# Batch 0's second exchange: by transposes for 8 of 32 m, through DRAM for the other 24

## The chip, the cores and the metric

One core of a Trainium2 chip runs the whole program. It has five engines that the profile names: TensorE (PE, with its weight loads as PEld), VectorE (DVE), ScalarE (ACT), GpSimd (POOL) and SyncE (SP, which only issues DMAs), and 16 DMA engines that all DMA queues share. PSUM, where TensorE writes, has eight banks of 2 KB for each of 128 partitions; only TensorE, VectorE and ScalarE reach it. The metric is the device time of one execution in microseconds (us), smaller is better.

## The reference, cut to what matters

```python
x:  (8, 3072, 256)            # batch, sequence, channel
X = rfft(x, axis=1);  Y = X * (filt_r + 1j * filt_i);  y = irfft(Y, n=3072, axis=1)
h = y.reshape(24576, 256)
g = maximum(h @ w1, h @ w2)   # (24576, 1024)
out = g @ w_out               # (24576, 256)
```

The Fourier transform of 3072 points is done as 96 times 32 with matrix products: sequence index = 32 p + m, with p from 0 to 95 and m from 0 to 31.

## The kernel before, in words

For each of the eight batches there are four matrix stages and then the feed-forward part.

- S1 contracts over p: the 96 rows of x are multiplied by the table C1 (`f1`, `s1`, and for batch 0 `s1t`). Its result has 96 rows, which are 24 frequencies u times 4 parts q.
- First exchange: from rows (u, q) and columns (m, d) to rows (q, m), 128 of them, for each u.
- S2 (`s2`) contracts over those 128 rows with the table U, for two pairs of u at a time: v = 0 to 5, each v covers four u and gives two PSUM banks px. `product` multiplies px with the filter F, giving two tiles pq for each v.
- S3 (`s3`) goes back with the tables VP and VQ, giving pz in rows (q, m) again.
- Second exchange: from rows (q, m) for each u to 96 rows (u, q) with columns (m, d), the tile zr.
- S4 (`s4`) contracts over the 96 rows with G1, for four m at a time, and leaves y transposed, with the channel on the partitions. One s4 makes one block tt of 384 tokens; a batch has eight blocks, and block i needs m = 4i to 4i+3.
- `moe_h` multiplies a block by Wd = w1 - w2 in eight steps j and takes the maximum with zero; `moe_o` multiplies the result by Wo and y by M = w2 Wo and adds them (max(a, b) = max(a - b, 0) + b).

For batches 1 to 7 both exchanges go through DRAM: `f1` or `s1` stores ad, and `f1_read` or `s1_read` reads it back as bt; `s3` stores zd, `z_read` reads it back as zr. For batch 0 both exchanges use TensorE transposes: `s1t` gives the result of S1 with the channel on the partitions, and `t1` turns it back as bt; `s3t` gives S3 with the channel on the partitions, as the tile zT with all 32 m, and `t2` turns four m of it at a time into zr.

The order of the work is written out by hand. First comes the opening: the tables (C1, U, VP, VQ) are made on the chip, x of batch 0 and the filter are loaded through GpSimd's queue, the second half of the filter's rows is doubled by VectorE (v below 4) or by DMA on SyncE's queue (v = 4, 5), and batch 0 goes through S1, S2, the products and S3. GpSimd makes some of the products (for s = 1 of v = 0, 2, 3, 4 and half of v = 5) from copies that ScalarE puts in SBUF (`stage_x`); after them stand on its queue the loads of batch 1's x, `prep_wd(0)` for Wd, the load of Wo (`load_wo`), another load of x and `prep_wd(1)`. Loads of w1 and w2 are on SyncE's queue. Matrix products of ones (`spin`, and one at the head of each `s3t`) fill waits of TensorE.

Then the main loop runs 64 steps for each batch, step = 8 tt + j. A step holds `moe_h(tt, j)`, a `visit` to the next batch from the list `mid` (S3 of the v before, S2 of this v, some S1 of the batch after next), about four products of `moe_o(tt - 1)`, and then whatever `todo` lists: f1, f1_read, t2, z_read, load_xf (x of a later batch, on SyncE's queue), fold (adds and subtracts its halves, GpSimd), casts and transposes of w2 (steps 3 to 7) and `prep_m` (step 8). At j = 4 (or 6 in the last block of a batch) the next block's s4 is issued, so s4(2) stands in step 12, s4(4) in step 28 and s4(8), the first of batch 1, in step 62.

Before, batch 0's t2 for c = 0 runs ahead of step 0, for c = 1 in step 2, and for c = 2 to 7 in steps 8, 16, 24, 32, 40 and 48. f1 for batch 1 runs once ahead of step 0 and 15 times in steps 0 to 12; f1_read stands in step 13, and batch 1's seven visits in steps 24, 28, 31, 35, 38, 42 and 46. Six PSUM banks belong to the pool ps and two to pso for the whole program. pq tiles come from pqpool (six) for v up to 2 and from pq0 (six more) for v from 3.

Of the kernel before, what the change touches and what calls it, by code (L numbers as in the profile page):

```python
# [8 lines left out]
FP32 = mybir.dt.float32  # L9
# [17 lines left out]
def kernel(  # L27
# [30 lines left out]
    zT = const.tile([128, 2, NM, NU, 4], BF16)  # L58
# [9 lines left out]
    ps = ctx.enter_context(tc.tile_pool(name="ps", bufs=6, space=bass.MemoryType.PSUM))  # L68
    pso = ctx.enter_context(tc.tile_pool(name="pso", bufs=2, space=bass.MemoryType.PSUM))
# [3 lines left out]
    pq0 = setup.enter_context(tc.tile_pool(name="pq0", bufs=6))  # L73
# [68 lines left out]

    V.memset(W1, 1.0)
# [3 lines left out]
    kc = init.tile([NP, NW, 2, 2], FP32)  # L147
    kap = init.tile([128, NW, 2], FP32)
# [3 lines left out]
    hv = init.tile([128, 2, 1], FP32)  # L152
    load_x(0, 0, 1)
    G.iota(pid, pattern=[[1, 1]], base=0, channel_multiplier=1, allow_small_or_imprecise_dtypes=True)
    G.iota(kc, pattern=[[2, NW], [24, 2], [1, 2]], base=0, channel_multiplier=0,
           allow_small_or_imprecise_dtypes=True)
    load_x(0, 1, 1)
    G.iota(kap, pattern=[[2, NW], [24, 2]], base=0, channel_multiplier=0,
# [4 lines left out]
    for c in range(3, 8):  # L163
        load_x(0, c, 1)
    for q in range(2):
        G.memset(hv[:, q], 1.0)
        for r in (0, 32):
            G.memset(hv[r:r + 1, q], 0.5 * (1 - q))
    load_f(0)
    load_f(1)  # L170
# [3 lines left out]
    def table_c():  # L174
        p96 = init.tile([128, 1], FP32)
        V.tensor_scalar(p96, pid, 1.0 / 96.0, None, OP.mult)
        uc = init.tile([NP, 48, 2], FP32)
        rc = init.tile([NP, 48, 2], FP32)
        kf = kc.rearrange("p w g s -> p (w g s)")
        V.tensor_scalar(uc[:, :, 0], kf, p96[0:NP], 0.25, OP.mult, OP.add)  # L180
        V.tensor_scalar(uc[:, :, 1], kf, p96[0:NP], None, OP.mult)
        V.tensor_scalar(uc[:, 0:1, 1], pid[0:NP], 0.5, 0.25, OP.mult, OP.add)
        V.tensor_scalar(rc, uc, RND, RND, OP.add, OP.subtract)
        V.tensor_tensor(uc, uc, rc, OP.subtract)
        S.activation(C1, uc.rearrange("p k r -> p (k r)"), AF.Sin, bias=zero[0:NP], scale=TWO_PI)
# [10 lines left out]
    def tables_u():  # L196
# [24 lines left out]
        V.tensor_scalar(t1[:, 0], kap.rearrange("p w g -> p (w g)"), a_, base, OP.mult, OP.add)  # L221
# [19 lines left out]
    def sines_u(h):  # L241
        uv = ua.rearrange("p u c s j -> p u (c s j)")
        S.activation(U[:, NW * h:NW * h + NW], uv[:, NW * h:NW * h + NW], AF.Sin, bias=zero, scale=TWO_PI)

    def table_g():
        pg = ps.tile([96, NP], FP32, tag="ps", name="pg")
        TE.matmul(pg, C1, I128[0:NP, 0:NP], start=True, stop=True)
        S.activation(G1, pg, AF.Copy)

    def table_v(h, q):  # L250
        pool, tag = (pso, "po") if h else (ps, "ps")
        pv = [pool.tile([128, 6, 64], FP32, tag=tag, name="pv%d" % s) for s in range(2)]
        for i in range(6):
            for g in range(2):
                for s in range(2):
                    rows = slice(64 * s, 64 * s + 64)
                    u = 2 * (6 * h + i) + g
                    if q == 0:
                        TE.matmul(pv[s][64 * g:64 * g + 64, i], U[rows, u], I128[rows, rows], start=True, stop=True)
                    else:  # L260
                        TE.matmul(pv[s][64 * g:64 * g + 32, i], U[rows, u, 32:64], I128[rows, rows],
                                  start=True, stop=True)
                        TE.matmul(pv[s][64 * g + 32:64 * g + 64, i], U[rows, u, 0:32], NI[rows, rows],
                                  start=True, stop=True)
        return pv

    def put_v(h, q, pv):
        for s in range(2):
            i0 = 1 if h == 0 and s == 0 else 0
            tab = VQ if q else VP  # L270
            if i0:
                S.activation(tab[:, 0, 0], pv[0][:, 0], AF.Identity, bias=zero, scale=hv[:, q])
            S.activation(tab[:, 6 * h + i0:6 * h + 6, s], pv[s][:, i0:6], AF.Copy)  # L273
# [96 lines left out]

    def s2(b, v):
        px = [ps.tile([128, 2, D], FP32, tag="ps", name="px%d" % s) for s in range(2)]
        for i in range(2):
            for s, g in ((0, 0), (1, 1), (0, 1), (1, 0)):
                u = 2 * (2 * v + i) + g
                TE.matmul(px[s][64 * g:64 * g + 64, i], U[64 * s:64 * s + 64, u], bt[b][64 * s:64 * s + 64, u],  # L376
                          start=True, stop=True)
        return px
# [12 lines left out]

    def s3(b, v, pq):
        if v == 0:
            zd[b] = dram.tile([NU, 128, D], BF16, tag="zd", name="zd")
        pz = [ps.tile([128, 2, D], FP32, tag="ps", name="pz%d" % g) for g in range(2)]
        for i in range(2):
            for q, tab in enumerate((VP, VQ)):
                for g, s in ((0, 0), (1, 1), (0, 1), (1, 0)):
                    TE.matmul(pz[g][64 * s:64 * s + 64, i], tab[64 * g:64 * g + 64, 2 * v + i, s],  # L399
                              pq[s][64 * g:64 * g + 64, q, i], start=(q == 0), stop=(q == 1))  # L400
        zt = zpool.tile([128, 2, 2, D], BF16, tag="zt", name="zt")
        for g in range(2):
            S.activation(zt[:, :, g], pz[g], AF.Copy)  # L403
        nc.sync.dma_start(out=zd[b][4 * v:4 * v + 4].rearrange("u p d -> p u d"),
                          in_=zt.rearrange("p i g d -> p (i g) d"))
# [89 lines left out]
    def s1t(c):  # L495
        for dc in range(2):
            pa = ps.tile([128, 4, 96], FP32, tag="ps", name="pa")
            for m in range(4):
                TE.matmul(pa[:, m], xb[0, c][:, m, 128 * dc:128 * dc + 128], C1, start=True, stop=True)
            o_ = at2[:, dc].rearrange("p u q m -> p (u q) m")[:, :, 4 * c:4 * c + 4]  # L500
            i_ = pa.rearrange("p m q -> p q m")
            if dc == 1 and c >= 6:
                V.tensor_copy(o_, i_)
            else:
                S.activation(o_, i_, AF.Copy)

    def t1(n, engine):
        pb = ps.tile([128, 4, D], BF16, tag="ps", name="pb")
# [9 lines left out]
    def s3t(v, pq):  # L518
        pool, tag = (ps, "ps") if v % 2 else (pso, "po")
        pz = [pool.tile([128, 2, 2, 2, 2, NM], FP32, tag=tag, name="pt%d" % g) for g in range(2)]  # L520
        for _ in range(2 if v == 1 else 1):
            TE.matmul(pz[0].rearrange("p i s r c m -> p (i s r c m)"), W1[:, 0:128], W1, start=True, stop=True)
        for i in range(2):
            for s in range(2):
                for dc in range(2):
                    for q, tab in enumerate((VP, VQ)):
                        for g in range(2):
                            TE.matmul(pz[g][:, i, s, :, dc], pq[s][64 * g:64 * g + 64, q, i, 128 * dc:128 * dc + 128],  # L528
                                      tab[64 * g:64 * g + 64, 2 * v + i, s].rearrange("p (r m) -> p r m", r=2),
                                      start=(q == 0), stop=(q == 1))  # L530
        zv = zT.rearrange("p c m (w g) q -> p w g (c m) q", g=2)
        for g in range(2):
            o_ = zv[:, 2 * v:2 * v + 2, g]
            i_ = pz[g].rearrange("p i s r c m -> p i (c m) (s r)")
            if v >= 4 and g == 1:
                V.tensor_copy(o_, i_)
            else:
                S.activation(o_, i_, AF.Copy)

    def t2(c, engines):  # L540
# [3 lines left out]
        for k, engine in enumerate(engines):  # L544
            pr = ps.tile([96, n, D], BF16, tag="ps", name="pr")
# [10 lines left out]
    def spin(n):  # L556
        for _ in range(n):
            pd = ps.tile([128, 512], FP32, tag="ps", name="pd")
            TE.matmul(pd, W1[:, 0:128], W1, start=True, stop=True)  # L559


    table_c()
# [8 lines left out]
    spin(12)  # L571
    for c in range(8):
# [3 lines left out]
        if c == 4:  # L576
            sines_u(0)
        if c < 7:
            spin(2)
    bt[0] = bpool.tile([128, NU, D], BF16, tag="bt", name="bt")  # L580
    for n in range(6):
        t1(n, S if n % 2 else V)
    put_v(0, 0, table_v(0, 0))
# [14 lines left out]
    def products(v):  # L598
        pool = pq0 if v > 2 else pqpool
# [5 lines left out]
        return pq  # L605

    pqs = {}
    pxs = {v: s2(0, v) for v in (1, 0)}
    stage_x(0)
    put_v(0, 1, table_v(0, 1))  # L610
    pxs[2] = s2(0, 2)
    stage_x(2)
    sines_u(1)
    put_v(1, 0, table_v(1, 0))
    pxs[3] = s2(0, 3)
    stage_x(3)
    put_v(1, 1, table_v(1, 1))
    for v in (1, 0, 2):
        pqs[v] = products(v)
    s3t(1, pqs[1])  # L620
    pxs[4] = s2(0, 4)
    stage_x(4)
    pqs[3] = products(3)
    s3t(0, pqs[0])
    pxs[5] = s2(0, 5)
    stage_x(5)
    for v in (2, 3):
        s3t(v, pqs[v])
    for v in (4, 5):
        pqs[v] = products(v)  # L630
    for v in (4, 5):
        s3t(v, pqs[v])
# [7 lines left out]
    setup.close()  # L640
    apool = ctx.enter_context(tc.tile_pool(name="apool", bufs=3))
# [4 lines left out]
    f1(1, 0, S)  # L646
    spin(1)
    t2(0, (V, S))
    spin(2)
    s4(0)  # L650
    spin(2)
# [7 lines left out]
    def plan_f1(b, nb, steps, read):  # L659
        for c, n in zip(range(1, 16), steps):  # L660
# [23 lines left out]
    for c in range(2, 8):  # L684
        plan(0, 8 * (c - 2) + 8, t2, c, (V,))
    plan_f1(0, 1, (0, 1, 1, 3, 4, 4, 5, 6, 6, 7, 8, 10, 11, 11, 12), 13)
    plan_f2(0, (24, 28, 31, 35, 38, 42, 46), ((0,), (1,), (2,), (3,), (4,), (5,), (6, 7)),
# [52 lines left out]
```

## Time and profile before

| | us |
|---|---|
| three runs, lowest, median, highest | 503.99, 504.77, 505.15 |
| the profiled execution | 503.8 |
| its span | 502.0 |
| TensorE, busy in the span | 488.4 |
| VectorE, ScalarE, GpSimd, busy | 331.9, 308.3, 257.5 |
| HBM read and written | 53.87 MB, 47.19 MB |
| issue of the load of Wo, and its landing | 37.19, 46.6 |
| start of batch 1's first s2 | 62.90 |

Times inside the span count from its start. The span is that of the instructions on the core; the execution's own time is 1.8 us longer. A busy TensorE is not TensorE at its peak, since matrix products are pipelined and their ends are modelled: the distance from one start to the next tells what one costs. A line such as "PE pr L549 x8" is eight instructions on TensorE of line 549 that write the tile pr. In a wait, the name after the arrow is what ended it. DMA shares of the profile can be slightly over 1.

### The profile page before, as it was taken

To read this page: it belongs to the slowest core of one execution; us is meant where nothing else is said; L and a number is where in the kernel's file an instruction comes from. 1 tells how busy PE (TensorE), PEld (TensorE's weight loads), DVE (VectorE), ACT (ScalarE), POOL (GpSimd) and SP (SyncE) were. 2 spreads that over 40 slices of the span, in tenths; PEclk is the share of its full clock that TensorE was granted. 3 is DMA by queue.
4 is the path that set the end of the run, shared out by engine and by line. 5 is a ranking of instruction groups with operands and counts; after the bars stand their busy time and mean duration, and the time that the engine had idled before them with its cause. 6 is when DMAs were issued, how large, how long until landed. Compare 5 with 4: busy or idle time off the path is not lost.

```text
span 502.0 us, 13079 instructions
## 1 busy us (share of the span) xinstructions
PE 488.4 (97%) x5299; PEld 362.1 (72%) x5303; DVE 331.9 (66%) x518; ACT 308.3 (61%) x629; POOL 257.5 (51%) x338
## 2 busy tenths in 40 slices
PE   8688999999999999999999999999999999999997
PEld 3455777777777777777777777777777777777775
DVE  7876688457865777457765687557765687555553
ACT  6776478647774676557764586647774465544442
POOL 7893569547463864645654855537632221222220
PEclk9989999999999999999999999999999999999999
DMA  7999789995799667986779558896769235411112
GB/s 125 150 252 217 230 229 290 306 274 171 212 268 260 175 204 234 250 229 189 198 244 275 187 177 245 235 239 197 197 181 255 78 111 153 168 65 64 64 64 84
DMA packets 77966, 97.20 MB, mean 194 GB/s; under 512 B 8017, under 2 KB 54354, under 8 KB 77842
## 3 DMA queue, kind: packets, MB, share of 16 engines
q1 hardware_dynamic: 64642, 66.73, 49.6%
q0 software_dynamic: 13264, 29.64, 20.3%
q8 instruction: 41, 0.67, 0.6%
q14 instruction: 19, 0.16, 0.1%
HBM read 53.87 MB, written 47.19 MB: 201 GB/s over the span
## 4 chain that ended last, share of the span: by engine, by line
PE 90%; DMA 5%; POOL 2%; issue 1%; ACT 1%; DVE 0%; SPq 0%; POOLq 0%; DVEq 0%
PE po L476 34%; PE ph L448 33%; PE po L474 8%; PE pz L399 5%; PE py L428 4%; PE pa L349 2%; DMA F<-in_filt_r_dram 2%; PE px L376 2%; DMA Wo<-in_moe_w_out_dram 2%; POOL xb L88 1%; DMA F<-F 1%; PE pr L549 1%; POOL pq L382 0%; PE pt L528 0%; PE pm__1132 L306 0%
## 5 line engine op out<-in xcount | busy, mean ns | idle before, releaser
L476 PE MATMUL po<-Wo,gt 128*128 128x256 bf16 x1536 | 261.0, 273 | 0.2 <-DMA Wo<-in_moe_w_out_dram 0.2
L452 ACT ACTIVATE gt<-ph 128x384 bf16<-128x384 f32 x321 | 157.0, 496 | 147.9 <-PE ph L448 147.3
L461 POOL DMA_DIRECT2D out_dram<-ot x186 | 102.6, 555 | 187.1 <-DVE ot L488 184.4
L476 PEld LDWEIGHTS <-gt 128*128 128x128 bf16 x1536 | 146.6, 98 | 66.1 <-issue 10.3
L450 DVE TENSOR_SCALAR gt<-ph 128x384 bf16<-128x384 f32 x191 | 104.9, 552 | 63.1 <-PE ph L448 59.9
L382 DVE TENSOR_TENSOR pq<-px,F 128x1024 bf16<-128x1024 f32 x91 | 107.0, 1219 | 24.2 <-PE px L376 22.6
L448 PEld LDWEIGHTS <-Wd 128*128 128x128 bf16 x1024 | 96.5, 98 | 12.9 <-POOL Wd L292 1.4
L103 POOL TENSOR_TENSOR xb<-XF 128x512 bf16<-128x512 f32 x48 | 61.2, 1276 | 41.3 <-DMA XF<-in_x_dram 21.2
L488 DVE COPY ot<-po 128x512 f32<-128x512 f32 x95 | 65.1, 685 | 25.3 <-PE po L476 25.0
L104 POOL TENSOR_TENSOR xb<-XF 128x512 bf16<-128x512 f32 x48 | 61.0, 1271 | 0.0
L403 ACT ACTIVATE zt<-pz 128x512 bf16<-128x512 f32 x84 | 45.6, 595 | 11.5 <-PE pz L399 8.4
L353 ACT ACTIVATE at<-pa 128x512 bf16<-128x512 f32 x96 | 51.8, 610 | 1.2 <-PE pa L349 0.8
L428 PE MATMUL py<-G,zr 96*128 96x96 bf16 x512 | 32.7, 206 | 0.2
L428 PEld LDWEIGHTS <-zr 96*128 96x128 bf16 x512 | 29.0, 97 | 2.5 <-DVE zr L552 0.4
L399 PE MATMUL pz<-pq,VP 64*64 64x256 bf16 x336 | 21.9, 281 | 0.0
L376 PE MATMUL px<-bt,U 64*64 64x256 bf16 x384 | 19.8, 278 | 1.2 <-ACT VQ L273 0.7
L399 PE MATMUL pz<-pq,VQ 64*64 64x256 bf16 x336 | 20.9, 269 | 0.0
L349 PE MATMUL pa<-xb,CT 64*64 64x512 bf16 x192 | 19.5, 383 | 0.0
L399 PEld LDWEIGHTS <-VP 64*64 64x64 bf16 x336 | 9.7, 105 | 13.3 <-issue 13.3
L376 PEld LDWEIGHTS <-U 64*64 64x64 bf16 x384 | 10.4, 109 | 3.9 <-issue 3.3
L559 PE MATMUL pd<-W 128*128 128x512 bf16 x30 | 10.5, 462 | 1.7 <-DVE zero L145 1.5
L552 DVE COPY zr<-pr 96x1024 bf16<-96x1024 bf16 (+1 forms) x8 | 5.2, 649 | 8.0 <-PE pr L549 8.0
(429 smaller groups left out, 609.7 us busy)
## 6 DMA issues: line engine op xcount, KB each, us to landing
out_dram<-ot POOLq DMA_DIRECT2D x186, 128.0 KB, 3.3
XF<-in_x_dram SPq DMA_DIRECT2D x96, 192.0 KB, 4.6
ad<-at SPq DMA_DIRECT2D x56, 192.0 KB, 3.3
bt<-ad SPq DMA_DIRECT2D x14, 768.0 KB, 9.1
zd<-zt SPq DMA_DIRECT2D x42, 256.0 KB, 2.7
zr<-zd SPq DMA_DIRECT2D x56, 192.0 KB, 4.8
WS<-in_moe_w_dram SPq DMA_DIRECT2D x4, 512.0 KB, 5.1
xb<-in_x_dram POOLq DMA_DIRECT2D x8, 192.0 KB, 5.8
```

What stands on the lines that cost most here:

```text
L103: G.tensor_tensor(t_[:, 0], f[:, 0], f[:, 1], OP.add)
L104: G.tensor_tensor(t_[:, 1], f[:, 0], f[:, 1], OP.subtract)
L353: S.activation(at[:, m0:m0 + 2], pa[g], AF.Copy)
L382: E.tensor_tensor(pq, px.rearrange("p (o i) d -> p o i d", o=1).to_broadcast([128, 2, 2, D]), F[:, :, 2 * v:2 * v + 2, s], OP.mult)
L399: TE.matmul(pz[g][64 * s:64 * s + 64, i], tab[64 * g:64 * g + 64, 2 * v + i, s], pq[s][64 * g:64 * g + 64, q, i], start=(q == 0), stop=(q ...
L428: TE.matmul(py[:, m], zr[b][:, 4 * i + m, 128 * dc:128 * dc + 128], G1, start=True, stop=True)
L448: TE.matmul(ph, Wd[:, dc, 128 * j:128 * j + 128], y_[:, dc], start=(dc == 0), stop=(dc == 1))
L450: V.tensor_scalar(gt[tt][:, j], ph, 0.0, None, OP.max)
L452: S.activation(gt[tt][:, j], ph, AF.Relu)
L461: E.dma_start(out=dst, in_=ot[tt // 2][:, 3 * (tt % 2) + c])
L476: TE.matmul(p_, g_[:, n - 2, blk], Wo[:, n - 2], start=(e == 0), stop=(e == 9))
L488: V.tensor_copy(ot[tt // 2][:, e - 1:e + 1], po[0])
```

## The change

The second exchange of batch 0 keeps its transposes for m = 0 to 7 only. zT shrinks from 32 m to 8, `s3t` multiplies by 16 columns of the tables where it had 64, and t2 remains for c = 0 and 1. For m = 8 to 31 batch 0 goes the way of the other batches: the plain S3 products (`s3_in`, 16 matrix products for each v), a store to zd (six stores of 256 KB, which hold all 32 m), and reads of three groups of eight m in two halves (`z_read0`, six DMAs, in step 2). The S3 of v = 0 to 3 (`s3_first`) stands between the stages of the opening, that of v = 4 and 5 (`s3_part`, `s3_out`) around t2(0) and s4(0), where spins and the first f1 were.

For the opening PSUM is divided otherwise: four single banks and two pairs of banks. `s1t`, `table_v`, `s3t` and `s3_first` write a pair, and one ScalarE instruction empties both banks. After the opening the pools ps and pso take the banks. So that the four u of a v lie next to each other, u is counted as 4v + 2g + i where it was 4v + 2i + g, and the factor one half of the special rows is multiplied into a copy of U (U0) by VectorE, where ScalarE scaled it when it emptied VP and VQ. The pool pq0 goes; all products of batch 0 use the six buffers of pqpool. The products at the head of `s3t` and five spins go.

In the main loop, t2 for c = 2 to 7 goes. f1 for batch 1 moves to steps 0, 1, 2, 3, 6, 8, 9, 11, 12, 14, 15, 17, 18, 19, 20 and 21, f1_read to step 22, and batch 1's visits to steps 29, 32, 35, 39, 42, 45 and 49 (z_read and s1_read, which are counted from them, move along).

```diff
-    zT = const.tile([128, 2, NM, NU, 4], BF16)
+    zT = const.tile([128, 2, 8, NU, 4], BF16)
...
-    pq0 = setup.enter_context(tc.tile_pool(name="pq0", bufs=6))
+    z0 = setup.enter_context(tc.tile_pool(name="z0", bufs=3))
+    single = setup.enter_context(tc.tile_pool(name="single", bufs=4, space=bass.MemoryType.PSUM))
+    pair = setup.enter_context(tc.tile_pool(name="pair", bufs=2, space=bass.MemoryType.PSUM))
...
     def put_v(h, q, pv):
-        for s in range(2):
-            i0 = 1 if h == 0 and s == 0 else 0
-            tab = VQ if q else VP
-            if i0:
-                S.activation(tab[:, 0, 0], pv[0][:, 0], AF.Identity, bias=zero, scale=hv[:, q])
-            S.activation(tab[:, 6 * h + i0:6 * h + 6, s], pv[s][:, i0:6], AF.Copy)
+        S.activation((VQ if q else VP)[:, 6 * h:6 * h + 6].rearrange("p i s m -> p s i m"), pv, AF.Copy)
...
+    def z_read0():
+        for m in range(8, NM, 8):
+            for h in range(2):
+                src = zd[0][12 * h:12 * h + 12].rearrange("u (q m) d -> (u q) m d", q=4)
+                nc.sync.dma_start(out=zr[0][48 * h:48 * h + 48, m:m + 8], in_=src[:, m:m + 8])
...
+    def s3_in(b, v, pz, pq, i):
+        for q, tab in enumerate((VP, VQ)):
+            for g, s in ((0, 0), (1, 1), (0, 1), (1, 0)):
+                TE.matmul(pz[g][64 * s:64 * s + 64, i], tab[64 * g:64 * g + 64, 2 * v + i, s],
+                          pq[s][64 * g:64 * g + 64, q, i], start=(q == 0), stop=(q == 1))
+
+    def s3_store(b, v, zt):
+        nc.sync.dma_start(out=zd[b][4 * v:4 * v + 4].rearrange("u p d -> p u d"),
+                          in_=zt.rearrange("p g i d -> p (g i) d"))
...
+    def s3_first(v, pq):
+        if v == 0:
+            zd[0] = dram.tile([NU, 128, D], BF16, tag="zd", name="zd")
+        t_ = two("pz").rearrange("p g (i d) -> p g i d", d=D)
+        for i in range(2):
+            s3_in(0, v, [t_[:, g] for g in range(2)], pq, i)
+        zt = z0.tile([128, 2, 2, D], BF16, tag="zt", name="zt")
+        S.activation(zt, t_, AF.Copy)
+        s3_store(0, v, zt)
...
+    def s3_out(v, g, engine):
+        if g == 0:
+            pz0[v, 2] = zpool.tile([128, 2, 2, D], BF16, tag="zt", name="zt")
+        if engine is S:
+            S.activation(pz0[v, 2][:, g], pz0[v][g], AF.Copy)
+        else:
+            V.tensor_copy(pz0[v, 2][:, g], pz0[v][g])
+        if g == 1:
+            s3_store(0, v, pz0[v, 2])
...
     def products(v):
-        pool = pq0 if v > 2 else pqpool
+        pool = pqpool
...
-    pxs = {v: s2(0, v) for v in (1, 0)}
+    pxs = {v: s2(0, v) for v in (0, 1)}
     stage_x(0)
-    put_v(0, 1, table_v(0, 1))
+    for h in range(2):
+        for q in range(2):
+            put_v(h, q, table_v(h, q))
+    products(0)
     pxs[2] = s2(0, 2)
     stage_x(2)
-    sines_u(1)
-    put_v(1, 0, table_v(1, 0))
+    products(1)
+    s3t(0, pqs[0])
     pxs[3] = s2(0, 3)
     stage_x(3)
-    put_v(1, 1, table_v(1, 1))
-    for v in (1, 0, 2):
-        pqs[v] = products(v)
     s3t(1, pqs[1])
+    products(2)
+    s3_first(0, pqs[0])
     pxs[4] = s2(0, 4)
     stage_x(4)
-    pqs[3] = products(3)
-    s3t(0, pqs[0])
+    products(3)
+    s3t(2, pqs[2])
+    s3_first(1, pqs[1])
     pxs[5] = s2(0, 5)
     stage_x(5)
-    for v in (2, 3):
-        s3t(v, pqs[v])
-    for v in (4, 5):
-        pqs[v] = products(v)
-    for v in (4, 5):
-        s3t(v, pqs[v])
+    products(4)
+    s3t(3, pqs[3])
+    s3_first(2, pqs[2])
+    products(5)
+    s3t(4, pqs[4])
+    s3_first(3, pqs[3])
+    s3t(5, pqs[5])
...
-    f1(1, 0, S)
-    spin(1)
-    t2(0, (V, S))
-    spin(2)
+    prs = [ps.tile([96, 2, D], BF16, tag="ps", name="pr")]
+    for v in (4, 5):
+        pz0[v] = [ps.tile([128, 2, D], FP32, tag="ps", name="pz%d" % g) for g in range(2)]
+    prs.append(ps.tile([96, 2, D], BF16, tag="ps", name="pr"))
+    for i in range(2):
+        s3_part(4, i)
+    t2(0, (V, S), prs)
+    s3_part(5, 0)
     s4(0)
-    spin(2)
+    s3_part(5, 1)
+    for g in range(2):
+        s3_out(4, g, V)
+    s3_out(5, 0, S)
+    s3_out(5, 1, V)
...
-    for c in range(2, 8):
-        plan(0, 8 * (c - 2) + 8, t2, c, (V,))
-    plan_f1(0, 1, (0, 1, 1, 3, 4, 4, 5, 6, 6, 7, 8, 10, 11, 11, 12), 13)
-    plan_f2(0, (24, 28, 31, 35, 38, 42, 46), ((0,), (1,), (2,), (3,), (4,), (5,), (6, 7)),
+    plan(0, 2, z_read0)
+    plan_f1(0, 1, (0, 1, 2, 3, 6, 8, 9, 11, 12, 14, 15, 17, 18, 19, 20, 21), 22)
+    plan_f2(0, (29, 32, 35, 39, 42, 45, 49), ((0,), (1,), (2,), (3,), (4,), (5,), (6, 7)),
```

## The prediction, made before the changed kernel was run

> **What bounds the kernel now.** I read the page's busy lines first, to see which engine could set the time at all.
>
> ```profile
> PE 488.4 (97%) x5299; PEld 362.1 (72%) x5303; DVE 331.9 (66%) x518; ACT 308.3 (61%) x629; POOL 257.5 (51%) x338
> PE   8688999999999999999999999999999999999997
> PEclk9989999999999999999999999999999999999999
> ```
>
> TensorE is full from the fifth slice (about 50 us) to the end. So only two things move the time: TensorE work that has to be done after about 50 us, and the waits before it. Table of stages next (columns: busy us of PE, PEld, DVE, ACT, POOL, then granted clock, DMA share, GB/s):
>
> ```profile
> 20.00:25.00 5.00, 2.47 (x111) 1.57 (x118) 4.47 (x5) 4.01 (x9) 4.93 (x5) 0.77 0.70 117
> 25.00:30.00 5.00, 4.53 (x128) 2.81 (x121) 4.57 (x5) 3.22 (x7) 5.00 (x3) 0.54 0.94 213
> 35.00:40.00 5.00, 4.34 (x39) 2.80 (x40) 2.81 (x6) 2.71 (x6) 4.99 (x4) 1.00 1.00 181
> 45.00:50.00 5.00, 4.47 (x43) 3.58 (x44) 1.42 (x3) 2.69 (x5) 0.00 (x0) 1.00 0.88 270
> 50.00:55.00 5.00, 5.00 (x44) 3.68 (x43) 3.86 (x8) 3.03 (x6) 0.00 (x0) 1.00 0.73 200
> ```
>
> Before 50 us GpSimd and the DMA engines are the full ones, not TensorE. The chain of work that ended last (start, us, what) says which of their pieces ends last:
>
> ```profile
> 30.64 2.10 POOL pq L382
> ...
> 37.19 9.41 DMA Wo<-in_moe_w_out_dram
> 46.64 0.60 PE po L476 x4
> 47.24 1.75 PE pm__1132 L306 x16
> 48.98 0.45 PE pr L549 x8
> ```
>
> GpSimd's products lead to the load of Wo; its landing at 46.6 opens step 8 (first output matmuls, prep_m, then transposes t2). Step 9 starts at 49.49. The DMA view of 36 to 42 us shows why Wo takes 9.4 us:
>
> ```profile
> q0 software_dynamic: 759, 1.00, 100.7%
> ad<-at SPq DMA_DIRECT2D x2, 192.0 KB, 8.6
> ```
>
> The GpSimd queue alone fills all 16 engines, and two stores of the SyncE queue need 8.6 us to land in it. Last, the timeline around batch 1's first exchange:
>
> ```profile
> 53.08 0.38 PE L324 MATMUL pa<-xb,C 96*96 96x512 bf16 x1
> ...
> 56.88 1.22 SPq L338 DMA_DIRECT2D bt<-ad  x2
> ...
> 62.90 0.41 PE L376 MATMUL px<-bt,U 64*64 64x256 bf16 x8
> ```
>
> The last f1 (step 12) runs at 53.08; its evacuation, the store of ad and the read of bt follow; batch 1's first s2 (step 24) starts 9.8 us later, and its weight load still waited 0.3 us for that DMA. So this exchange has no slack today.
>
> **The sum, part by part**, against the profiled execution's own 503.8 us (span 502.0; the median of the runs shown, 504.77, stands 1.0 above it).
>
> 1. Removed: t2 for c = 2 to 7, 0.45 each in the chain. One lies in step 8 (term 4); five lie in the full stretch: -2.25.
>
> 2. f1 moves later. Before, c0 to c11 run by step 8 and c12 to c15 after it; now c0 to c5 by step 8 and ten after. From one start to the next an f1 takes 0.22 (43.13 to 43.35), so six more in the full stretch: +1.3. Terms 1 and 2: -0.9 after step 8.
>
> 3. The opening's products. Twelve pq buffers (pqpool and pq0) become six, and pxs has four banks where it had six. GpSimd's product of v=3 now waits for s3_first(0). VectorE has the products of v=0 and 1 done at 27.4 (23.8 and three of 1.2); then TensorE must do s2(3), s3t(1) and s3_first(0): 0.6, 0.95 and 1.1 at half clock, about 2.0 if the clock has recovered by its end. That starts GpSimd at 29.4 to 30.0; 2.13, 2.13 and 1.16 follow, ending at 34.9 to 35.5 where it was 33.88. The load of Wo and both prep_wd stand behind on GpSimd's queue. I take +1.0 (0 to +1.6).
>
> 4. The zd stores: six of 256 KB, new in this stretch, on SyncE's queue. The nearest row with 512-byte rows is the bt read between 55 and 64 us:
>
> ```profile
> q1 hardware_dynamic: 3297, 1.93, 72.6%
> ```
>
> 1.93 MB in 72.6% of 9 us is 0.295 MB per us, so a store is 0.9 us of all engines and six are 5.3. The first drains behind the w1/w2 loads. Of the rest, if half pass before Wo's last byte: +2.3 (0 if the GpSimd queue holds them off as it held off ad; 4.5 if all five pass). I take the middle, since both queues have work waiting. Wo lands at 46.64 + 1.0 + 2.3 = 49.9. Then 0.44 (first outputs), 1.75 (prep_m), 0.22 (f1): step 9 at 52.3 instead of 49.49, +2.8, the t2 of term 1 included.
>
> The Trainium skill (DMA: Bandwidth & Descriptors, Queues, rings and completion order) says that an engine takes the queues in turn, a whole packet of up to 64 descriptors at a time. By it the stores alternate with Wo as I assumed; the 8.6 us of ad bear more on one queue going first. By that row the Wo term would be 0, and all of the delay would move to term 5.
>
> 5. z_read0. s4(2), at step 12, needs m = 8 to 15, read from zd after all six stores have landed. Step 12 would come at 52.3 and 3.6 (four steps of 0.76, two f1) = 55.9. The remaining stores land about 52.4; a read of zd lands 4.4 at least after issue: 57.0. +1.1 (0 to +4.5). If the stores are held until Wo is in, Wo lands at 47.6, but the stores end about 53 and the read near 57.5: the same place by another way. SyncE waits at z_read0 from step 2 on; ad stores and XF loads of batch 2 queue behind it, which the shift of f1 allows for.
>
> 6. Batch 1's read. The last f1 is now at step 21 and s2(1) at step 29. Eight steps took 6.66 (55.82 to 62.48) with one t2; take off that 0.45 and one step of 0.76, add the matmul pair of step 29 (0.33) and the f1 (0.22): 6.0 us between them, where the exchange took 9.8 before. By the smallest rows it takes 0.4 + 0.69 (evacuation) + 0.32 (issue) + 2.1 (ad lands) + 0.4 + 5.8 (bt lands) = 9.7. TensorE takes its work in order, so all stands: +3.5 after the 0.3 it waited already (+2.8 to +11, the latter with the 13.3 that another bt read took). XF loads (load_xf(2,3), (2,4)) are queued on SyncE ahead of the last stores and of the read, and they wait for folds, so an end below 2.8 is not likely.
>
> 7. Clock. The wait for Wo leaves TensorE idle for some 3.4 us, and the fillers in s3t and five spins are gone. In 20 to 25 us a busy share of half brought the clock to 0.77, then 0.54. Half speed for some 3.4 us costs 1.7; I take half, +0.8 (0 to 1.7).
>
> The Trainium skill (TensorE: Matmul & The Clock Gate, Part 1) has the gate close after an idle window of about 3.4 us. By it this term is 0 or the whole price, not half.
>
> 8. Hidden edits. ScalarE's two-bank copies: rows of 384, 512 and 1024 elements cost 0.49, 0.60 and 1.02, so 768 cost about 0.81, 0.17 less than two of 384; but s1t waits for x to land, so nothing is gained. Six s3 (0.56 each) replace fillers in TensorE's waits. Four copies of 1.02 on ScalarE answer ten of 0.60 that halve. s3_out puts three casts of 0.69 on VectorE ahead of the first ph evacuations, covered by the wait for Wd (41.07) and Wo; if Wo were early, they would cost up to 1. Three memsets fewer on GpSimd let the filter loads be issued up to 0.5 earlier, but later ones wait for x's DMAs: 0. Batch 1's last visit moves three steps towards s4(8); its read landed near 99.5 for 102.17, so 0.4 is left: 0 (to +1.5).
>
> Sum: 2.8 + 1.1 + 3.5 - 0.9 + 0.8 = +7.3, so 511.1 by the profiled execution and 512.1 by the median; I put **511.5**.
>
> **Rivals.**
> - *The stores are absorbed.* They drain in gaps of the weight loads and after Wo. Then terms 4, 5 and 7 go: step 8 is set by GpSimd (+1.0) and by w2T, with six f1 fewer in front, so -0.5; with -0.9 and +3.5 that is +2.1: **506.4**, between the two sums as before (505 to 508). For it: DMA share 0.70 to 0.94 in 20 to 30. Against: 1.00 in 35 to 40.
> - *The exchange lands in time* (the other side). Place: s2(1) at step 29. If ad and bt land so fast on emptier engines that term 6 is gone, and the stores are absorbed for the same reason, -0.5 and -0.9 stay, with the 0.3: -1.7, **502.6**, again between the two. It decides from where all waits together are under 0.4 us, so store and read would have to land within 4.6 us; the smallest rows sum to 7.9. That speaks against it; f1 spread over more steps speaks for it.
> - *The queue locks up.* SyncE stands at z_read0, then at load_xf behind late folds, and the bt read takes 13.3: **519**.
>
> **How the numbers follow.** Forecast 0.55 (507 to 517), stores absorbed 0.20, in time 0.15, lock-up 0.10. No change means within 0.2%, 1.0 us, about what a measurement of this kernel can tell. Of the in-time case 0.13 is faster and 0.02 same; of the absorbed one 0.06 is same: faster 0.13, same 0.08, slower 0.79. The range 502.5 to 517 leaves out half of the in-time case and the lock-up.
>
> **What would show it.** Wo landing after 49 us; a wait of TensorE at s4(2)'s weights for zr and at s2(1)'s for bt, the latter over 2.5 us; GpSimd's last product ending after 34.5; a lower granted clock between 45 and 55. No wait at s2(1), or Wo before 47.5, would make the forecast wrong.

## The result and the profile after

The changed kernel takes **517.31 us** (median of six, 514.1 to 518.75) beside 504.63 for the kernel before on the same chip (six runs): ratio 1.0243, interval 1.021 to 1.0277. The forecast was 511.5: the direction was right, the loss is 12.7 us where about 7 were expected, and the median lies 0.3 above the upper end of the range, 517. The profiled execution took 517.8, with a span of 516.0 (502.0 before).

The same lines as before: the page's busy time and slices, then the table of stages (columns as above).

```profile
PE 492.3 (95%) x5339; PEld 364.2 (71%) x5339; DVE 329.8 (64%) x514; ACT 308.3 (60%) x617; POOL 256.0 (50%) x335
PE   8577987999999999999999999999999999999996
PEclk9856997999999999999999999999999999999999
```

```profile
20.00:25.00 5.00, 1.41 (x101) 1.14 (x93) 4.86 (x5) 2.90 (x4) 3.82 (x4) 0.78 0.88 143
25.00:30.00 5.00, 4.66 (x139) 3.19 (x142) 4.47 (x4) 3.15 (x6) 4.09 (x3) 0.50 0.86 227
35.00:40.00 5.00, 2.53 (x62) 1.86 (x55) 0.52 (x2) 1.02 (x1) 4.97 (x5) 0.50 1.12 262
45.00:50.00 5.00, 3.00 (x15) 1.88 (x15) 2.73 (x5) 1.80 (x4) 0.00 (x0) 0.67 1.03 251
50.00:55.00 5.00, 4.13 (x43) 2.85 (x42) 3.18 (x7) 3.90 (x7) 0.00 (x0) 0.99 0.66 175
```

Two things are new. TensorE's granted clock is 0.50 in 35 to 40 and 0.67 in 45 to 50, where it was 1.00 in both; and TensorE is listed busy for only 2.53 and 3.00 of 5 us there. The chain of work that ended last (start, us, what) names what was waited for, and it is not Wo:

```profile
28.81 1.03 ACT zt L434
29.86 7.34 DMA zd<-zt
37.30 1.03 ACT zt L434
38.35 8.00 DMA zd<-zt
46.46 0.50 ACT gt L497
...
54.49 0.44 PE po L521 x4
54.93 1.84 PE pm__1195 L310 x16
...
70.23 2.31 DMA ad<-at
72.61 7.34 DMA bt<-ad
79.99 0.64 PE px L389 x7
```

And the waits for DMAs between 24 and 85 us (total, times, longest):

```profile
PE px L389 <- DMA bt<-ad: 4.8, 1, 4.8
ACT gt L497 <- DMA zd<-zt: 3.4, 1, 3.4
ACT zt L434 <- DMA zd<-zt: 2.8, 1, 2.8
DVE gt L495 <- DMA zd<-zt: 2.2, 1, 2.2
```

What to see: two stores of zd, 7.34 and 8.00 us from issue to landing, hold ScalarE up. The first holds the fourth zt, since the pool z0 has three buffers for four stores. The second holds the first gt of the main loop: gt lies where z0 lay, because z0 was released with the opening's memory, and a buffer that a DMA still reads cannot be written. Neither wait was in the prediction. The third wait, batch 1's read of bt, was.

The DMA view of 36 to 42 us answers the one before:

```profile
q0 software_dynamic: 262, 0.80, 74.7%
q1 hardware_dynamic: 1095, 0.54, 32.2%
...
Wo<-in_moe_w_out_dram POOLq DMA_DIRECT2D x1, 512.0 KB, 9.4
...
zd<-zt SPq DMA_DIRECT2D x1, 256.0 KB, 8.0
```

Wo is issued 0.6 later than before (37.79) and takes the same 9.4 us, while the SyncE queue, which holds zd, has 32% of the engines beside it. Wo landed at 47.2 and opened nothing: the first output product starts at 54.49.

Where the 14.0 us of the span arise is read from the start of the first ph of each block tt (before, after): tt = 0 37.48, 42.36; tt = 1 (step 8) 45.97, 54.01; tt = 2 55.82, 63.38; tt = 3 62.48, 70.70; tt = 4 72.52, 84.42; tt = 8 103.17, 116.72. So the shift is +4.9 when the main loop begins, +8.0 at step 8, +7.6 at tt = 2, +8.2 at tt = 3, +11.9 behind the late read and +13.6 from tt = 8 on. The 11.9 is not a loss alone: two visits that stood ahead of tt = 4 (steps 28 and 31) are still to come there, and three t2 of 0.45 that stood behind it are gone. From tt = 8 on TensorE is nearly full in both kernels, and nothing is made up.

### The profile page after: what moved, and what is told of

Its sections match the earlier page's. It is cut to its first block, busy times and chain, and to the rows that moved or that the text cites. A ratio compares the mean times of both kernels' runs of the same rounds, so it can differ in the third digit from the quotient of the medians.

```text
span 516.0 us, 13167 instructions
## 1 busy us (share of the span) xinstructions
PE 492.3 (95%) x5339; PEld 364.2 (71%) x5339; DVE 329.8 (64%) x514; ACT 308.3 (60%) x617; POOL 256.0 (50%) x335
## 4 chain that ended last, share of the span: by engine, by line
PE 88%; DMA 7%; DVE 2%; POOL 1%; ACT 1%; issue 0%; POOLq 0%; ACTq 0%; SPq 0%; DVEq 0%
PE po L521 33%; PE ph L493 32%; PE po L519 8%; PE pz L408 5%; PE py L473 4%; DMA zd<-zt 3%; PE pa L353 3%; PE px L389 2%; DMA xb<-in_x_dram 2%; DMA bt<-ad 1%; DVE F L130 1%; DVE pq L395 1%; POOL xb L88 1%; PE pa L328 1%; DMA F<-in_filt_i_dram 1%; DMA ad<-at 0%
## 5 line engine op out<-in xcount | busy, mean ns | idle before, releaser
L408 PE MATMUL pz<-pq,VP 64*64 64x256 bf16 x384 | 27.1, 298 | 3.4 <-ACT zt L434 3.4
L408 PE MATMUL pz<-pq,VQ 64*64 64x256 bf16 x384 | 26.2, 287 | 0.0
L408 PEld LDWEIGHTS <-VP 64*64 64x64 bf16 x384 | 12.2, 110 | 16.9 <-issue 15.6
L408 PEld LDWEIGHTS <-VQ 64*64 64x64 bf16 x384 | 12.1, 113 | 0.0
L353 PEld LDWEIGHTS <-CT 64*64 64x64 bf16 x192 | 8.8, 106 | 2.9 <-ACT gt L497 1.2
```

## The experiments

Each is compared with the kernel before on its own chip. Theory: the loss is a sum of delays in several places (the two zd waits, the late read, the clock in the opening), and each can be taken away. Rival: one bound stands behind them, the queue of SyncE or the 16 DMA engines, and what one edit frees is lost at the next transfer. Where an edit names `kept`, z0 is made beside zrpool, outside the opening's memory.

**A fourth buffer.**

```diff
-    z0 = setup.enter_context(tc.tile_pool(name="z0", bufs=3))
+    z0 = setup.enter_context(tc.tile_pool(name="z0", bufs=4))
```

> z0 with four buffers instead of three, still in the memory of the opening. Theory 1 (two waits on zd stores, and the late read of bt): ScalarE's wait of 2.8 us at the fourth zt goes, s4(0) comes some 2.5 us earlier; but the first gt still lies on memory of z0 and waits for a store to land, so only part is gained: 514 to 517, the wait of gt for zd above 2 us. Rival (the opening is bound by GpSimd's Wd and by the load of Wo, the waits on stores lie beside them): no change, 517. Third (no overlap of gt and z0, the gt wait is only a late fourth store): 512.

Measured 516.9, ratio 1.0274 (1.0223 to 1.0325), no better than the change itself. The time alone cannot tell theory 1 from the rival. The waits can: that at the fourth zt is gone, and the one behind it grew from 3.4 to 4.3:

```profile
ACT gt L497 <- DMA zd<-zt: 4.3, 1, 4.3
PE px L389 <- DMA bt<-ad: 3.6, 1, 3.6
```

**z0 outside the opening's memory, still three buffers.**

```diff
     zrpool = ctx.enter_context(tc.tile_pool(name="zrpool", bufs=2))
+    z0 = ctx.enter_context(tc.tile_pool(name="z0", bufs=3))
...
-    z0 = setup.enter_context(tc.tile_pool(name="z0", bufs=3))
```

> z0 with three buffers, but in memory that is kept after the opening, so that no later tile lies on it. Theory 1: the wait of the first gt for zd (3.4 us on ScalarE, 2.2 on VectorE) is gone, the wait of 2.8 at the fourth zt stays; step 9 some 3 us earlier, 513 to 515. If gt's wait had another cause it is still there, 517.

Measured 514.25, ratio 1.0199 (1.0172 to 1.0225). gt no longer waits for zd, though zt still does (2.8). Step 8 starts at 50.56 instead of 54.01, and the span is 3.0 shorter. So of the two waits, that for the memory of gt is the one that set the opening's end; the fourth buffer alone had brought step 8 only to 53.02.

**Both: four buffers, kept.**

> z0 with four buffers in kept memory: neither wait. Theory 1: no wait of ScalarE or VectorE for zd before 50 us, step 9 at about 49.6 (Wo lands near 47.2 and opens step 8, as before the change) where it was 56.8; the late read of bt stays: 509 to 511. The forecast's term (the stores delay Wo): Wo lands at 49 or later and step 9 starts after 52: 512 to 514.

Measured 514.07, ratio 1.0192 (1.0167 to 1.0217): by the medians the two zd waits together are worth about 2.7 of the 12.7. The profiled run, 511.99, was the fastest of the four, so its trace shows more gain than that. Wo landed at 46.3, so the forecast's term (Wo at 49 or later) is out here too, and 509 to 511 was not reached either. TensorE, VectorE and ScalarE wait for a DMA at only one more place, TensorE at bt (4.7), yet step 8 still starts at 48.73, 2.8 late, and the granted clock is 0.50 until about 43. The chain shows what the opening runs by then:

```profile
32.98 1.03 ACT zt L434
34.02 0.04 issue
34.06 1.09 PE pz L408 x14
35.15 0.02 issue
35.17 1.03 ACT zt L434
36.20 0.04 issue
36.25 1.07 PE pz L408 x16
```

TensorE and ScalarE take turns: s3_first writes one of only two pairs of banks, ScalarE empties both banks in one instruction of 1.03, and the next s3_first, which needs this pair, waits. At half clock one round is 2.2 us (32.98 to 35.17).

**f1 and the read at the steps of before, in the changed kernel.**

```diff
-    plan_f1(0, 1, (0, 1, 2, 3, 6, 8, 9, 11, 12, 14, 15, 17, 18, 19, 20, 21), 22)
+    plan_f1(0, 1, (0, 0, 1, 1, 3, 4, 4, 5, 6, 6, 7, 8, 10, 11, 11, 12), 13)
```

> The changed kernel with f1 and f1_read of batch 1 in the steps of the kernel before (c0 in step 0 as well), the visits left at 29 to 49. Theory 1: TensorE does not wait for bt (4.8 us), its clock does not fall at 80 us (1.7 of half speed), and six f1 go back into waits (1.3): 509 to 511. Rival (f1's copies in steps 0 to 8 delay the steps, which is why they were moved): 514 or more.

Measured 513.63, ratio 1.019 (1.0137 to 1.0242), which lies between the theory's range and the rival's; the profiled run took 517.27, the longest of four. There the wait for bt is gone and tt = 4 starts at 74.24, only 1.7 behind the kernel before, with the two visits of steps 28 and 31 still to come. In that run the gain is then lost: tt = 8 starts at 114.17, 11.0 behind, and there are new waits at batch 1's second exchange:

```profile
PE py L473 <- DMA zr<-zd: 3.7, 1, 3.7
ACT zt L423 <- DMA zd<-zt: 3.1, 1, 3.1
```

**The kernel before with the late plan alone** (f1 in steps 1 to 21, read in 22, visits from 29; t2 kept).

> The kernel before with only the plan of the changed one: f1 in steps 1 to 21, read in 22, visits from 29; everything else as before, t2 included. Theory (the late read costs by itself what it cost in the changed kernel): a wait of 3 to 5 us for bt at the first s2 of batch 1, the clock lower just behind it, +4.5 to +7 us on the kernel before. The sum of the prediction for this step alone: +3.5. Rival (the read is late only because the zd stores and reads stand ahead of it on the SyncE queue): less than +2.

Measured 510.09, ratio 1.0106 (1.0044 to 1.0169): +6.4 by the medians, +4.2 by its profiled run of 508.0.

```profile
PE px L376 <- DMA bt<-ad: 2.6, 1, 2.6
```

So the late plan is a loss by itself, without any zd store or read of batch 0 in the way. Its rival, under 2, is out. The prediction's own terms for this plan, +1.3 for six more f1 in the full stretch and +3.5 for the wait, make +4.8. One part of the theory missed: the clock did not fall behind the wait (1.00 in 65 to 85).

**Four kept buffers and the whole plan of before** (f1, read, and visits from 24).

> Four zt buffers that outlive the opening, and batch 1's f1, read and visits at the steps of the kernel before (f1 in steps 0 to 12, read in 13, visits from 24). Theory (two separate delays: a slow opening worth some 3 us at step 8, and the late read worth some 5 us and a fall of the clock): TensorE does not wait for bt at the first s2 of batch 1 by more than 0.5 us, step 8 stays near 49 us, and the time falls from 514.1 to 506 to 508.5. Rival (the SyncE queue is the bound: what the read gains is lost at the next transfer of that queue, as when the early f1 stood alone): 511 to 514, with a wait of over 2 us for batch 1's zr or zd.

Measured 511.65, ratio 1.0151 (1.0088 to 1.0215); its profiled run took 514.65, the longest of four. The time lies in the rival's range; its sign, a wait of over 2 us for batch 1's zr or zd, did not come. Instead TensorE waits 3.5 us for bt again, and the timeline of SyncE's queue shows what delayed the read:

```profile
46.70 8.48 SPq L379 DMA_DIRECT2D zr<-zd  x6
55.28 1.33 SPq L336 DMA_DIRECT2D ad<-at  x3
56.66 0.45 SPq L93 DMA_DIRECT2D XF<-in_x_dram  x1
...
62.70 0.86 SPq L336 DMA_DIRECT2D ad<-at  x2
66.83 1.29 SPq L342 DMA_DIRECT2D bt<-ad  x2
```

SyncE stands at batch 0's first read of zd, 5.9 us of it waiting for the last stores of zd; three stores of ad and then the loads of x queue behind. In the changed kernel the reads were issued from 48.19, with 2.0 us of such waiting.

**Products of ones against the half clock.** Twelve stand ahead of the second s2, two at the head of each s3t; the plan is the changed one.

```diff
             put_v(h, q, table_v(h, q))
+    pd = two("pd")
+    for _ in range(12):
+        TE.matmul(pd[:, 0], W1[:, 0:128], W1, start=True, stop=True)
```

> Four zt buffers that outlive the opening, the changed plan of f1 and visits, and products of ones back in the opening: twelve ahead of the second s2 (where TensorE waits 2.9 us for VectorE) and two at the head of each s3t. Theory (the opening is late because TensorE runs at a granted clock of 0.50 from 25 to 43 us): the clock is back at 1.00 by 32 us, the first output products start near 46.5 to 47.5 instead of 49.2, and the time falls by 1.5 to 3 from 514.1. Rival (GpSimd's products and the DMAs set the opening, the clock only fills their waits): the clock rises and the first output products stay at 49 or later, time 513.5 to 515.

Measured 514.57, ratio 1.0195 (1.0138 to 1.0252), in the rival's range. The clock is 1.00 from 20 to 35 as wanted, and s3t(5) runs at 34.45. Then TensorE stands still in the middle of it:

```profile
34.45 0.44 PE pz L577 x28
34.89 3.90 issue
38.78 0.23 PE pz L577 x4
```

Nothing that the profile knows is waited for: the four products that follow use the same tiles as the 28 ahead of them. The clock then falls back to 0.50 from 40 to 46, and the loop starts at 43.49, later than without fillers (40.23). So this run can't say what the half clock costs by itself.

**Fillers, kept buffers and the plan of before.**

> Both: four kept zt buffers, the products of ones, and the plan of the kernel before. Theory (the delays add): 503 to 506, within 0.5% of the kernel before. Rival (one bound behind all): 509 or more.

Measured 511.36, ratio 1.0126 (1.005 to 1.0202). The rival's range again: it is the same as without fillers (511.65), with a stand in the same place of s3t(5), here 2.3, and the same wait for bt (3.5).

**Batch 0's reads of zd on GpSimd's queue** (four kept buffers, plan of before).

```diff
-                nc.sync.dma_start(out=zr[0][48 * h:48 * h + 48, m:m + 8], in_=src[:, m:m + 8])
+                G.dma_start(out=zr[0][48 * h:48 * h + 48, m:m + 8], in_=src[:, m:m + 8])
```

> Four kept zt buffers, the plan of the kernel before, and batch 0's six reads of zd issued by GpSimd instead of SyncE. Theory (SyncE's order: while it stands 6 us at the first read of zd, the stores of ad and the loads of batch 2's x wait behind it, and so the read of bt): the stores of ad follow their f1 within 2 us, TensorE waits less than 0.5 us for bt, and the time falls from 511.7 to 506 to 508.5. Rival (the DMA engines are full, and whatever is issued earlier lands later): the wait for bt stays over 2.5 us, 510.5 to 513.

Measured 511.1, ratio 1.0138 (1.0095 to 1.0181). SyncE's stand at the read of zd is gone, and ad's last store is issued at 57.62 instead of 63.17 (the kernel with four kept buffers and the whole plan of before). But it now takes far longer to land:

```profile
57.62 6.76 DMA ad<-at
...
64.53 4.58 DMA bt<-ad
...
69.14 0.41 PE px L389 x8
```

It took 3.59 there. So what was issued 5.6 us earlier landed only 2.4 us earlier, and the wait for bt is still 2.5. The rival's time and wait came.

**The first four stores of zd on ScalarE's queue**, in the changed kernel.

```diff
-        nc.sync.dma_start(out=zd[b][4 * v:4 * v + 4].rearrange("u p d -> p u d"),
+        (nc.scalar if b == 0 and v < 4 else nc.sync).dma_start(out=zd[b][4 * v:4 * v + 4].rearrange("u p d -> p u d"),
```

> The changed kernel, with only the first four stores of zd issued from ScalarE's own DMA queue instead of SyncE's. Theory (a store takes 7 to 8 us because it stands behind the loads of w1 and w2 in SyncE's queue): each store lands within 5 us, the two waits for zd (fourth zt, first gt) fall from 2.8 and 3.4 us to under 1 each, and the time from 517.3 to 513.5 to 515.5, as with the two memory edits. Rival (the 16 DMA engines are full between 28 and 46 us, and no queue is faster): landings of 6.5 to 8 us, both waits stay, 516 to 519.

Measured 517.83, ratio 1.0284 (1.022 to 1.0348). The stores on the chain still take 7.00 and 7.42, and both waits stay (1.8 and 2.9). So their place behind the w1 and w2 loads in SyncE's queue is not what made them slow.

**The first loads of batch 2's x behind the read of bt** (on top of the reads by GpSimd).

```diff
-            (6, 10, 14, 18, 21, 25, 29, 33), (14, 18, 21, 25, 28, 32, 36, 40))
+            (13, 14, 16, 18, 21, 25, 29, 33), (20, 22, 24, 26, 28, 32, 36, 40))
```

> The last kernel but one of this study (four kept zt buffers, plan of the kernel before, reads of zd issued by GpSimd) with the first loads of batch 2's x moved behind the read of bt: steps 13, 14, 16, 18 instead of 6, 10, 14, 18, their folds to steps 20, 22, 24, 26. Theory (the DMA engines are over 0.85 busy from 25 to 70 us, so a transfer that is taken out of the way makes the stores of ad and the read of bt land earlier): the last store of ad lands within 4 us of its issue where it took 6.8, the wait for bt falls from 2.5 us to under 0.5, time 507 to 509.5. Rival (the loads of x only fill gaps): the wait for bt stays over 2 us, 510.5 to 513, or a visit waits for a fold.

Measured 521.23, ratio 1.0333 (1.0309 to 1.0357). This kernel has a fault: XF has three buffers, and the load for c = 3 in step 18 stands ahead of the fold for c = 0 in step 20, so part of batch 2's x is replaced by another part. For the waits it can still be read. The last store of ad landed in 4.07 us instead of 6.76, the read of bt went out 3.2 us earlier (61.36 against 64.53), and the wait fell from 2.5 to 1.1. So the loads of x do cost the exchange time. In return S1 of batch 2 waits 13.0 us for its fold:

```profile
PE pa L353 <- POOL xb L103: 13.0, 1, 13.0
```

**No zd transfers for batch 0** (four kept buffers, plan of before; stores and reads left out, GpSimd fills zr).

> Four kept zt buffers and the plan of the kernel before, but batch 0's S3 result is neither stored to zd nor read back: six stores and six reads are left out, and GpSimd fills zr for m = 8 to 31 with ones. So batch 0's output is not the reference's; TensorE, VectorE and ScalarE do all that they did. Theory (the 2.7 MB of new transfers are the price: they hold up Wo, ad, bt and SyncE): no wait for bt over 0.5 us, step 8 near 47 us, time 503 to 505.5. Rival (the order of the opening, its half clock and its smaller matrix products are the price, the transfers only show it): step 8 stays at 48.5 us or later, time 507 to 510.

Measured 508.21, ratio 1.0072 (1.0052 to 1.0091): 3.9 above the kernel before, where the same kernel with the transfers was 8.0 above it, so 4.1 less. The wait for bt is gone (0.3). The loop starts at 40.14, where it started at 40.23 with four kept buffers and the transfers, and at 37.48 in the kernel before: these 2.7 us belong to the opening and not to the transfers. The result lies in the rival's range, but the filling brought a cost of its own, as VectorE's instructions show:

```profile
44.42 0.68 DVE L596 COPY zr<-pr 96x1024 bf16<-96x1024 bf16 x1
45.02 2.67 DVE L289 CAST w2b<-WS 128x512 bf16<-128x512 f32 x1
47.61 0.54 DVE L495 TENSOR_SCALAR gt<-ph 128x384 bf16<-128x384 f32 x1
48.07 0.41 DVE L289 CAST w2b<-WS 128x512 bf16<-128x512 f32 x1
```

The first cast, from SBUF to SBUF, runs into GpSimd's fills (42.11 to 47.4) and takes 2.67 instead of 0.41; the copy ahead of it, which reads PSUM, takes its usual 0.68 beside the same fills. The Trainium skill (SBUF — State Buffer, SBUF: two separate sides) says that VectorE and GpSimd share one pair of ports, and that a GpSimd instruction and a VectorE instruction in a mode that needs both ports lock each other out for a whole instruction; the 2.3 us here agree, though no view names the cast's mode. The cast stands on the chain to step 8, which came at 51.96; with the transfers and the same plan it came at 52.63 (in the longest of four runs), and at 50.13 with the reads on GpSimd's queue. If all 2.3 reached the end, the transfers cost about 6.4 of those 8.0 us. That is an estimate; the run itself shows 4.1.

## Why the prediction was right or wrong

The direction held, and the mechanism of one term; the largest part came from somewhere else. That the total came as near as 5.8 us is partly luck: 3.9 of the 7.3 forecast (terms 4 and 5) were put on waits that did not come, and waits that the forecast did not have stood in their place.

- *Terms 1 and 2 (five t2 against six f1, -0.9)*: their prices can be read where nothing waits. From tt = 2 to tt = 3 the changed kernel has five f1 more and one t2 less, +0.65 by the prediction's prices, and the stretch grew by 0.66 (6.66 to 7.32). Their sum over the whole stretch can't be read, because the visits move as well.
- *Term 3 (opening's products, +1.0)*: GpSimd's last product ended at 34.49 instead of 33.88, +0.6, inside its 0 to 1.6. But the term took GpSimd for the end of the opening. With the zd waits gone the chain runs through s3_first and ScalarE's zt by turns, on two pairs of banks, and the loop starts 2.7 us late.
- *Term 4 (Wo, +2.8 at step 9)*: **this step failed.** Wo landed at 47.2, not 49.9. The shift at step 9 was +7.3 (56.83 against 49.49). In its place the runs showed two waits on the buffers that the stores read, and a later opening at half clock behind them. Without the wait for gt's memory step 8 came 3.4 us earlier (54.01 to 50.56 with z0 kept), without both waits 5.3 (48.73); of the time the medians show 2.5 and 2.7. The term asked who shares the DMA engines with the stores; it should also have asked what a store holds while it runs: its source buffer, and later the memory that is released under it.
- *Term 5 (z_read0 and s4(2), +1.1)*: no wait. The reads were issued from 48.19 to 52.8, and s4(2) came only at 60.58, because the opening was so late. With the old plan the other half of the term appeared: SyncE stands 5.9 us there, and the stores of ad queue behind it.
- *Term 6 (bt, +3.5; its own numbers, 9.7 less 6.0 less 0.3, give 3.4)*: right place and mechanism; the wait was 4.8 in the changed kernel and 2.6 with the late plan alone, on either side of the forecast. The 6.0 us of work between the last f1 and s2(1) came out as said (69.22 to 75.2). The landing of bt was the size that was off: 7.34 where the smallest row, 5.8, had been used.
- *Term 7 (clock, +0.8)*: the stretch was far too short. The clock was 0.50 or 0.67 over all of 25 to 50, not for 3.4 us, and lower again behind the read (0.74 and 0.58 in 75 to 85). What that costs in time no run shows by itself.
- *Term 8 (hidden edits, 0)*: the fillers of s3t and the spins were counted as free to remove. They were part of what kept the clock up (with fillers it was 1.00 from 20 to 35); but putting fillers back gave nothing, and TensorE then stood 3.9 us.
- *Rivals.* "Absorbed" (506.4) was half right: Wo was not delayed. "In time" (502.6) is out. "The queue locks up" (519) is nearest in time; its long stand of SyncE (5.9 us) was seen only with the old plan, and what made the time in the changed kernel was something else.

Of the listed signs, a wait at s2(1) over 2.5 (4.8) and a lower clock between 45 and 55 (0.67, then 0.99) came; Wo after 49 and a wait at s4(2) did not, and GpSimd's last product ended just short of its mark (34.49 for 34.5). That Wo before 47.5 would make the forecast wrong was one of the prediction's own conditions, and it came true: Wo landed at 47.2.

What stays open: why TensorE stands in s3t(5) when its clock is up. In each of the two runs the DMA view shows one instruction load of 20 KB among data that keep the engines full, in 36 to 37 us where the stand is 34.89 to 38.78, and in 34 to 35 where it is 35.08 to 37.37. So a late instruction load is a candidate; no run took the load off to test it. Open too is what the half clock costs: in the run with the loads of x behind the read the clock happened to be 1.00 from 31 to 34.6, and the loop started at 40.37, against 40.84 in the same kernel without that move. The split of the last 8 us is known only within the bounds above: 4.1 shown for the transfers, 2.7 of late loop without them, and a cast that GpSimd's fills made slow. No kernel with the change beats the one before; the nearest that compute everything took 511.1 and 511.4 (ratios 1.0138 and 1.0126).

## What to carry to other kernels

For a store that is moved early, list what it holds until it lands: the buffers of its pool against the stores in flight, and every tile that will be placed on that memory once the pool is released. Here that cost some 3 us in a place that no queue or bandwidth count points to. Where the DMA engines are nearly full for 40 us on end, as here, moving a transfer to another queue (7.0 and 7.4 us where it took 7.3 and 8.0) or issuing it earlier (6.8 where it took 3.6) gained little or nothing in these runs; fewer bytes, and other transfers moved out of the way, did make room.

## What the runs showed of the hardware that was not expected

- TensorE was listed busy for 4.66, 4.46 and 4.40 of 5 us in three stretches from 25 to 40 (four kept buffers), and its granted clock stayed at 0.50 throughout:

```profile
25.00:30.00 5.00, 4.66 (x143) 3.30 (x140) 4.28 (x4) 3.41 (x7) 4.09 (x3) 0.50 0.96 235
30.00:35.00 5.00, 4.46 (x119) 3.28 (x111) 3.05 (x3) 3.43 (x7) 4.83 (x5) 0.50 1.01 326
35.00:40.00 5.00, 4.40 (x84) 3.02 (x80) 1.01 (x3) 2.11 (x3) 4.97 (x5) 0.50 1.12 253
```

  In the kernel before, whose s3t has products of 64 columns and a filler of 512 where the changed one has 16 columns alone, the clock was 1.00 from 30 on after 4.53 busy in 25 to 30. The Trainium skill (TensorE: Matmul & The Clock Gate, Part 1) has the gate open after one busy window of about 3.4 us; by that, as an estimate, the clock would have been up by 34 at the latest, two such windows after 27. The measurement decides: it was not. Nor is it a fixed rule of this work: in the run with the loads of x behind the read, with the same opening, it was up from 31 to 34.6 and at 0.50 again from 35 to 40. That small products count for less is one reading; it is not shown, since no run varied the size alone.
- TensorE can stand for 2.3 to 3.9 us between products of one group with no semaphore in play, while the DMA engines are full. The Trainium skill (Runtime: NRT & Kernel Launch, Instruction fetch mechanics) calls the streaming of instructions mostly hidden; if this is such a load, it is not hidden here.
- The stores of zd on the chain, 256 KB each, took 7.0 to 8.0 us to land between 29 and 46 us, from SyncE's queue and from ScalarE's alike. With fillers in the opening one took 16.8. Over the whole program the median of such a store is 2.6.
